# Linear attention followed by a gated feed-forward layer on one core: the kernel rewritten with one 512-token block per batch, larger loads, Silu, and an instruction order fixed by hand

## The chip, the cores and the metric

The kernel runs on one core of a Trainium2 chip. The metric is the device time of one execution in microseconds (us). Before the change the median of three runs was 443.9 us (439.84 to 444.03). A profile is one further execution, recorded by the hardware profiler. Its span runs from the first to the last instruction and is usually a little shorter than the timed execution. TensorE multiplies matrices (PE in the profile, and PEld for its weight loads), VectorE (DVE), ScalarE (ACT) and GpSimd (POOL) do the elementwise work, and SyncE (SP) issues the stores.

## The reference, cut to what matters

There are 8 batches, 8 heads, 576 tokens and 64 columns per head. So the feed-forward layer gets 8 x 576 = 4608 tokens of 512 columns, and works with 2048 hidden columns.

```python
def phi(x): return np.where(x > 0, x, np.exp(x) - 1.0) + 1.0
q_p, k_p = phi(q), phi(k)
kv  = np.einsum('bhsd,bhse->bhde', k_p, v)
z   = np.sum(k_p, axis=2)
num = np.einsum('bhsd,bhde->bhse', q_p, kv)
den = np.einsum('bhsd,bhd->bhs', q_p, z)[..., None] + 1e-06
x   = (num / den) transposed to tokens x 512      # abridged
h   = x @ w_in                                    # 512 -> 2048
g   = h * sigmoid(beta * h)                       # written out in the original
y   = g @ w_out                                   # 2048 -> 512, float32
```

phi(x) equals max(x, 0) + min(exp(x), 1). Both kernels use a form of this. Also, h * sigmoid(beta h) = silu(beta h) / beta. The changed kernel uses that.

## The kernel before

The kernel handles one batch of attention, then one block of 512 tokens of the feed-forward layer, and so on. Batches have 576 tokens and blocks 512, so a ninth block is left at the end. A scheduler orders the instructions of each engine. The parts that matter here:

```python
# weights: converted to bf16 by the DMA, issued on GpSimd's queue
nc.gpsimd.dma_start(out=w_in_sb, in_=moe_w_in...)
nc.gpsimd.dma_start(out=w_out_sb, in_=moe_w_out...)
...
# one load per 128 tokens and tensor: every written run is 64 columns of bf16, 128 bytes
nc.gpsimd.dma_start(out=qk[:sn, 0], in_=q_src[s0:s0 + sn])
...
# attention: per head pair and token tile one small normalization
nc.vector.reciprocal(rden[:sn], num_ps[:sn, :, D])
nc.vector.tensor_mul(xtile[:sn], num_ps[:sn, :, :D], rden_v)      # 128 x 128
nc.tensor.matmul(xtp[:, sc, :], xtile..., identity, is_transpose=True, ...)
...
# the block: two PSUM buffers for h_ps, two for y_ps
for ff in range(FFC):                                   # 16
    for kc in range(DMC): nc.tensor.matmul(h_ps, w_in_sb[...], xT_sb[...], ...)   # 4
    nc.scalar.activation(sig, h_ps, Sigmoid, scale=beta_sb[:, ff : ff + 1])
    nc.vector.tensor_mul(g_sb[:, ff, :], h_ps, sig)
for tsub in range(TB // P):                             # 4
    for ff in range(FFC): nc.tensor.matmul(y_ps, g_sb[...], w_out_sb[:, ff, :], ...)  # 16
    nc.vector.tensor_copy(y_sb, y_ps)
    nc.sync.dma_start(out=out[...], in_=y_sb)
```

Of the kernel before, what the change touches and what calls it, by code (L numbers as in the profile page):

```python
# [10 lines left out]
BF16 = mybir.dt.bfloat16  # L11


@with_exitstack
def kernel(
# [10 lines left out]
    nc = tc.nc  # L26

    B, H, S, D = q.shape
    DMODEL = H * D
    NTOK = B * S  # L30
    DFF = moe_w_in.shape[1]
    P = 128
    DMC = DMODEL // P
    FFC = DFF // P
    SC = (S + P - 1) // P
    SP = SC * P

    assert moe_w_in.shape == (DMODEL, DFF)
    assert moe_w_out.shape == (DFF, DMODEL)
    assert out.shape == (NTOK, DMODEL)  # L40
    assert DMODEL % P == 0 and DFF % P == 0

    consts = ctx.enter_context(tc.tile_pool(name="consts", bufs=1))

    identity = consts.tile([P, P], BF16)
    make_identity(nc, identity)

    w_in_sb = consts.tile([P, DMC, DFF], BF16)
    w_out_sb = consts.tile([P, FFC, DMODEL], BF16)
    beta_sb = consts.tile([P, FFC], F32)  # L50
    with tc.high_priority(offset=-100000):
        nc.gpsimd.dma_start(out=w_in_sb, in_=moe_w_in.rearrange("(c p) f -> p c f", p=P))
        nc.gpsimd.dma_start(out=w_out_sb, in_=moe_w_out.rearrange("(c p) f -> p c f", p=P))
        for ff in range(FFC):
            nc.sync.dma_start(out=beta_sb[:, ff : ff + 1],
                              in_=moe_beta[ff * P : (ff + 1) * P, None])

    kvmask = consts.tile([P, 2, D + 1], BF16)
    nc.gpsimd.memset(kvmask, 0.0)
    nc.gpsimd.memset(kvmask[:D, 0, :], 1.0)  # L60
    nc.gpsimd.memset(kvmask[D : 2 * D, 1, :], 1.0)

    xT_sb = consts.tile([P, DMC, NTOK], BF16)

    atp = ctx.enter_context(tc.tile_pool(name="attn", bufs=3))
    attn_batch = ctx.enter_context(tc.tile_pool(name="attn_batch", bufs=2))
    psA = ctx.enter_context(tc.tile_pool(name="psA", bufs=2, space=bass.MemoryType.PSUM))
    kvnps = ctx.enter_context(tc.tile_pool(name="kvnps", bufs=2, space=bass.MemoryType.PSUM))
    moe_sb = ctx.enter_context(tc.tile_pool(name="moe_sb", bufs=3))
    moe_g = ctx.enter_context(tc.tile_pool(name="moe_g", bufs=2))  # L70
    hps = ctx.enter_context(tc.tile_pool(name="hps", bufs=2, space=bass.MemoryType.PSUM))
    yps = ctx.enter_context(tc.tile_pool(name="yps", bufs=2, space=bass.MemoryType.PSUM))

    def phi_to(dst, src, tag):
        shape = list(src.shape)
        mn = atp.tile(shape, BF16, tag=tag + "_mn")
        nc.vector.tensor_scalar(mn, src, 0.0, None, mybir.AluOpType.min)  # L77
        ex = atp.tile(shape, BF16, tag=tag + "_ex")
        nc.scalar.activation(ex, mn, mybir.ActivationFunctionType.Exp)  # L79
        rl = atp.tile(shape, BF16, tag=tag + "_rl")  # L80
        nc.scalar.activation(rl, src, mybir.ActivationFunctionType.Relu)  # L81
        nc.vector.tensor_add(dst, rl, ex)  # L82

    def attention_batch(b):
        q_pT = attn_batch.tile([P, DMC, SP], BF16, tag="q_pT")
        qk_p_all = attn_batch.tile([P, SC, 2, DMODEL], BF16, tag="qk_p_all")
        v_all = attn_batch.tile([P, SC, H, D + 1], BF16, tag="v_all")
        nc.gpsimd.memset(v_all[:, :, :, D : D + 1], 1.0)

        q_src = q[b].rearrange("h s d -> s h d")  # L90
        k_src = k[b].rearrange("h s d -> s h d")
        v_src = v[b].rearrange("h s d -> s h d")

        for sc in range(SC):
            s0 = sc * P
            sn = min(P, S - s0)

            qk = atp.tile([P, 2, H, D], BF16, tag="qk")
            if sn < P:
                nc.gpsimd.memset(qk[sn:P], -50.0)  # L100
            nc.gpsimd.dma_start(out=qk[:sn, 0], in_=q_src[s0:s0 + sn])  # L101
            nc.gpsimd.dma_start(out=qk[:sn, 1], in_=k_src[s0:s0 + sn])  # L102
            qkv = qk.rearrange("p a h d -> p (a h d)")
            qk_p_sc = qk_p_all[:, sc].rearrange("p a f -> p (a f)")
            phi_to(qk_p_sc, qkv, tag="phi_qk")
            q_p = qk_p_all[:, sc, 0, :]
            tps = psA.tile([P, SC, P], BF16, tag="trps")
            for dmc in range(DMC):
                nc.tensor.matmul(  # L109
                    tps[:, dmc, :], q_p[:, dmc * P : (dmc + 1) * P], identity,  # L110
                    is_transpose=True, start=(dmc == 0), stop=(dmc == DMC - 1),
                    skip_group_check=True,
                )
            nc.vector.tensor_copy(q_pT[:, :, s0 : s0 + P], tps[:, :DMC, :])

            nc.gpsimd.dma_start(out=v_all[:sn, sc, :, :D], in_=v_src[s0:s0 + sn])  # L116
            if sn < P:
                nc.gpsimd.memset(v_all[sn:P, sc, :, :D], 0.0)
        k_p_all = qk_p_all[:, :, 1, :]

        tok0 = b * S
        for p in range(DMC):
            dlo = p * P
            kv01 = kvnps.tile([P, 2 * (D + 1)], F32, tag="kvn")
            for sc in range(SC):
                nc.tensor.matmul(
                    kv01,
                    k_p_all[:, sc, dlo : dlo + P],
                    v_all[:, sc, 2 * p : 2 * p + 2].rearrange("s h e -> s (h e)"),
                    start=(sc == 0),  # L130
                    stop=(sc == SC - 1),
                )

            kv_bd = atp.tile([P, 2, D + 1], BF16, tag="kv_bd")
            nc.vector.tensor_mul(kv_bd, kv01.rearrange("p (g e) -> p g e", g=2), kvmask)  # L135

            xtp = psA.tile([P, SC, P], BF16, tag="trps")
            for sc in range(SC):
                s0 = sc * P
                sn = min(P, S - s0)  # L140

                num_ps = kvnps.tile([P, 2, D + 1], F32, tag="kvn")
                nc.tensor.matmul(  # L143
                    num_ps.rearrange("p g e -> p (g e)"),
                    q_pT[:, p, s0 : s0 + P],
                    kv_bd.rearrange("p g e -> p (g e)"),
                    start=True,
                    stop=True,
                )
                rden = atp.tile([P, 2], F32, tag="rden")  # L150
                nc.vector.reciprocal(rden[:sn], num_ps[:sn, :, D])  # L151
                xtile = atp.tile([P, 2, D], BF16, tag="xtile")
                rden_v = rden[:sn, :, None].to_broadcast([sn, 2, D])
                nc.vector.tensor_mul(xtile[:sn], num_ps[:sn, :, :D], rden_v)  # L154
                if sn < P:
                    nc.vector.memset(xtile[sn:P], 0.0)
# [83 lines left out]
```

## Time and profile before

| | before |
|---|---|
| time, median | 443.9 us |
| span of the profile | 443.6 us |
| TensorE, VectorE, ScalarE busy | 77%, 57%, 54% |
| mean granted clock of TensorE | 0.942 |
| first h product / first copy of y | 59.7 / 112.5 us |
| DMA packets | 122,619, of which 115,424 under 512 B |

TensorE is the engine to watch. Its time goes in three ways: products that run at full rate, products that run at a reduced clock, and waits. The prediction below shows the lines. In a group line (the page's costliest groups), the parts are: source line, engine, operation, out<-in with shapes, count | busy us, mean ns | idle time before, and what ended most of it.

VectorE copies y out of PSUM four times per block, so the start of each block's last copy dates the end of that block. For the kernel before these ends are 125.3, 179.4, 209.6, 239.1, 295.3, 323.6, 365.1, 410.2 and 439.7 us.

### The profile page before, as it was taken

Reading aid. Unit: us, or ns where it says so; the run is one execution under the profiler, and the core shown is the slowest. Engines: PE = TensorE matmul, PEld = TensorE weight load, DVE = VectorE, ACT = ScalarE, POOL = GpSimd, SP = SyncE. Lnnn points to the kernel's source line nnn. Section 1 sums busy time; section 2 is a strip of 40 time slices with the busy share of each in tenths; the row PEclk is TensorE's granted clock in tenths of the full one; section 3 lists DMA queues with packets and bytes.
Section 4 is the critical chain, followed back from the end, with each engine's and each line's share of the span. In section 5 each row is a group of like instructions: output and inputs, shape, how many; then the busy total and the mean of one; then the engine's idle time right before and its main releaser. Section 6 shows DMA issues by size and latency. Waiting matters only on the chain.

```text
span 443.6 us, 5178 instructions
## 1 busy us (share of the span) xinstructions
PE 341.9 (77%) x1760; PEld 160.0 (36%) x1792; DVE 253.0 (57%) x716; ACT 238.2 (54%) x272; POOL 118.9 (27%) x155
## 2 busy tenths in 40 slices
PE   0256366377877768989998677899988997899996
PEld 0134123133343333434444333444434444244342
DVE  1699538408387687453554858735467537453551
ACT  2764539839789999740551998525103500341540
POOL 9998618202813463300002534000000000000000
PEclk9999999679989899999999988999979996699999
DMA  9999999917997497901002958020110010001002
GB/s 80 110 130 110 186 103 108 184 12 47 137 95 48 31 96 86 104 0 73 24 8 90 99 37 55 1 95 0 49 47 2 0 71 25 0 0 73 24 1 95
DMA packets 122619, 28.14 MB, mean 63 GB/s; under 512 B 115424, under 2 KB 117472, under 8 KB 122592
## 3 DMA queue, kind: packets, MB, share of 16 engines
q0 software_dynamic: 115104, 18.36, 57.1%
q1 hardware_dynamic: 7488, 9.45, 6.1%
q8 instruction: 14, 0.23, 0.2%
q14 instruction: 13, 0.11, 0.1%
HBM read 36.71 MB, written 9.44 MB: 104 GB/s over the span
## 4 chain that ended last, share of the span: by engine, by line
PE 55%; DMA 16%; DVE 15%; POOL 6%; issue 4%; ACT 4%; DVEq 0%; POOLq 0%; ACTq 0%
PE y_ps L193 26%; PE h_ps L176 25%; DMA qk<-in_k_dram 9%; DMA w_out_sb<-in_moe_w_out_dram 4%; DVE g_sb L188 3%; DMA w_in_sb<-in_moe_w_in_dram 3%; DVE xtile L154 3%; POOL qk L101 2%; POOL v_all L116 2%; DVE mn L77 2%; ACT sig L184 2%; DVE rden L151 2%; PE xtp L157 2%; DVE qk_p_all L82 1%; DVE xT_sb L162 1%
## 5 line engine op out<-in xcount | busy, mean ns | idle before, releaser
L184 ACT ACTIVATE sig<-h_ps,beta_sb 128x512 bf16<-128x512 f32 x144 | 96.6, 686 | 147.2 <-PE h_ps L176 134.9
L176 PE MATMUL h_ps<-xT_sb,w_in_sb 128*128 128x512 bf16 x554 | 150.2, 401 | 25.1 <-DVE g_sb L188 18.8
L193 PE MATMUL y_ps<-w_out_sb,g_sb 128*128 128x512 bf16 x566 | 143.2, 387 | 12.7 <-DMA w_out_sb<-in_moe_w_out_dram 9.7
L188 DVE TENSOR_TENSOR g_sb<-h_ps,sig 128x512 bf16<-128x512 f32 x144 | 96.8, 686 | 52.9 <-ACT sig L184 52.8
L176 PEld LDWEIGHTS <-w_in_sb 128*128 128x128 bf16 x576 | 57.9, 101 | 99.4 <-issue 44.1
L193 PEld LDWEIGHTS <-g_sb 128*128 128x128 bf16 x576 | 56.0, 100 | 84.5 <-issue 16.4
L157 PE MATMUL xtp<-identity,xtile 128*128 128x128 bf16 x160 | 35.3, 254 | 27.7 <-DVE xtile L154 26.9
L79 ACT ACTIVATE ex<-mn 128x1024 bf16<-128x1024 bf16 x40 | 41.8, 1053 | 20.6 <-DVE qk_p_all L82 10.7
L101 POOL DMA_DIRECT2D qk<-in_q_dram x40 | 34.8, 869 | 59.4 <-ACT rl L81 50.0
L201 DVE COPY y_sb<-y_ps 128x512 f32<-128x512 f32 x36 | 24.6, 689 | 45.5 <-PE y_ps L193 45.4
L81 ACT ACTIVATE rl<-qk 128x1024 bf16<-128x1024 bf16 x40 | 41.9, 1051 | 11.6 <-DMA qk<-in_k_dram 11.6
L154 DVE TENSOR_TENSOR xtile<-num_ps,rden 128x128 bf16<-128x128 f32 (+1 forms) x160 | 41.3, 283 | 1.1 <-DVE rden L151 0.2
L143 PE MATMUL num_ps<-kv_bd,q_pT 128*128 128x130 bf16 x160 | 32.3, 254 | 9.3 <-DVE kv_bd L135 9.3
L151 DVE RECIPROCAL rden<-num_ps 128x2 f32<-128x2 f32 (+1 forms) x160 | 22.1, 160 | 28.0 <-PE num_ps L143 26.1
L157 PEld LDWEIGHTS <-xtile 128*128 128x128 bf16 x160 | 16.5, 103 | 56.7 <-DVE xtile L154 47.2
L77 DVE TENSOR_SCALAR mn<-qk 128x1024 bf16<-128x1024 bf16 x40 | 20.2, 508 | 28.1 <-DMA qk<-in_k_dram 28.0
L116 POOL DMA_DIRECT2D v_all<-in_v_dram x40 | 35.7, 907 | 0.0
L109 PE MATMUL tps<-identity,qk_p_all 128*128 128x128 bf16 x160 | 17.8, 245 | 22.9 <-DVE qk_p_all L82 20.3
L102 POOL DMA_DIRECT2D qk<-in_k_dram x40 | 34.7, 867 | 1.3 <-DMA qk<-in_q_dram 0.8
L184 ACT ACT_TABLE_LOAD x24 | 30.8, 1283 | 4.9 <-PE h_ps L176 4.1
L82 DVE TENSOR_TENSOR qk_p_all<-rl,ex 128x1024 bf16<-128x1024 bf16 x40 | 26.9, 680 | 6.1 <-ACT ex L79 5.9
L79 ACT ACT_TABLE_LOAD x23 | 29.5, 1283 | 0.4
(23 smaller groups left out, 123.4 us busy)
## 6 DMA issues: line engine op xcount, KB each, us to landing
out_dram<-y_sb SPq DMA_DIRECT2D x36, 256.0 KB, 2.0
qk<-in_q_dram POOLq DMA_DIRECT2D x32, 128.0 KB, 4.3
qk<-in_k_dram POOLq DMA_DIRECT2D x32, 128.0 KB, 4.6
v_all<-in_v_dram POOLq DMA_DIRECT2D x32, 128.0 KB, 4.7
w_in_sb<-in_moe_w_in_dram POOLq DMA_DIRECT2D x1, 2048.0 KB, 13.9
w_out_sb<-in_moe_w_out_dram POOLq DMA_DIRECT2D x1, 2048.0 KB, 16.2
qk<-in_q_dram POOLq DMA_DIRECT2D x8, 64.0 KB, 3.6
qk<-in_k_dram POOLq DMA_DIRECT2D x8, 64.0 KB, 3.7
```

Of the source, the lines that this page charges most:

```text
L79: nc.scalar.activation(ex, mn, mybir.ActivationFunctionType.Exp)
L81: nc.scalar.activation(rl, src, mybir.ActivationFunctionType.Relu)
L101: nc.gpsimd.dma_start(out=qk[:sn, 0], in_=q_src[s0:s0 + sn])
L102: nc.gpsimd.dma_start(out=qk[:sn, 1], in_=k_src[s0:s0 + sn])
L116: nc.gpsimd.dma_start(out=v_all[:sn, sc, :, :D], in_=v_src[s0:s0 + sn])
L143: nc.tensor.matmul(num_ps.rearrange("p g e -> p (g e)"), q_pT[:, p, s0 : s0 + P], kv_bd.rearrange("p g e -> p (g e)"), start=True, stop=True,)
L154: nc.vector.tensor_mul(xtile[:sn], num_ps[:sn, :, :D], rden_v)
L157: nc.tensor.matmul(xtp[:, sc, :], xtile.rearrange("s g e -> s (g e)"), identity, is_transpose=True, start=(sc == 0), stop=(sc == SC - 1), ...
L176: nc.tensor.matmul(h_ps, w_in_sb[:, kc, ff * P : (ff + 1) * P], xT_sb[:, kc, t0 : t0 + TB], start=(kc == 0), stop=(kc == DMC - 1),)
L184: nc.scalar.activation(sig, h_ps, mybir.ActivationFunctionType.Sigmoid, scale=beta_sb[:, ff : ff + 1],)
L188: nc.vector.tensor_mul(g_sb[:, ff, :], h_ps, sig)
L193: nc.tensor.matmul(y_ps, g_sb[:, ff, tsub * P : (tsub + 1) * P], w_out_sb[:, ff, :], start=(ff == 0), stop=(ff == FFC - 1),)
```

## The change

The intent is to keep TensorE fed from the start:

- Each block is the first 512 tokens of one batch. The 64 odd tokens of all eight batches make the ninth block.
- The weights are loaded right after batch 0. q, k and v come in whole batches with written runs of 512 bytes (1 KB read).
- Silu writes g in one step, and 1/beta is multiplied into w_out once.
- h and y share four PSUM buffers.
- Normalization is done for 512 columns at once.
- The order of the instructions is written out by hand: generators hand out one step of the next batch's attention after each group of four large products.

The diff has 522 lines. This is its core (cuts marked with "..."):

```diff
+    ctx.enter_context(tc.manual_schedule())
+    mmps = ctx.enter_context(tc.tile_pool(name="mmps", bufs=4, space=bass.MemoryType.PSUM))
-    hps = ctx.enter_context(tc.tile_pool(name="hps", bufs=2, space=bass.MemoryType.PSUM))
-    yps = ctx.enter_context(tc.tile_pool(name="yps", bufs=2, space=bass.MemoryType.PSUM))
...
+        nc.gpsimd.dma_start(
+            out=dst[:, :, 0:NJ, :].rearrange("p h j d -> p h (j d)"),
+            in_=src[b, :, 0:MAIN, :].rearrange("h (p j) d -> p h (j d)", j=NJ),
+        )
...
-            sig = moe_sb.tile([P, TB], BF16, tag="sig")
-            nc.scalar.activation(
-                sig, h_ps, mybir.ActivationFunctionType.Sigmoid,
-                scale=beta_sb[:, ff : ff + 1],
-            )
-            nc.vector.tensor_mul(g_sb[:, ff, :], h_ps, sig)
+            nc.scalar.activation(
+                g[:, ff, :], hp, ACTF.Silu, scale=beta_c[:, ff : ff + 1]
+            )
+            step(fill)
...
-                nc.vector.reciprocal(rden[:sn], num_ps[:sn, :, D])
-                nc.vector.tensor_mul(xtile[:sn], num_ps[:sn, :, :D], rden_v)
+            nc.vector.tensor_scalar(den[:n], nv[:, :, :, D], 1e-6, None, ALU.add)
+            nc.vector.reciprocal(rden[:n], den[:n])
+            nc.vector.tensor_mul(
+                xs[t][:n], nv[:, :, :, 0:D],
+                rden[:n, :, :, None].to_broadcast([n, 2, 4, D]),
+            )
...
-    for b in range(B):
-        attention_batch(b)
-        moe_block(b)
-    moe_block(B)
+    h_phase(0, xT[0], [chain(wait(4), w_out_scale())])
+    clear_tail(2)
+    load_next(2)
+    f = chain(wait(6), lazy(elu, 1), wait(3), lazy(attention, 1))
+    y_phase(0, [f])
+    drain(f)
+    load_next(3)
+    h_phase(1, xT[1])
+    f = chain(lazy(elu, 2), lazy(attention, 2))
+    e3 = chain(wait(8), lazy(elu, 3))
+    y_phase(1, [f, e3])
...
+    for b in range(2, B + 1):
+        att = lazy(attention, b + 1) if b + 1 < B else wait(0)
+        h_phase(b, xT[b % 3] if b < B else xT_tail, [att])
+        load_next(b + 3)
+        e = lazy(elu, b + 2) if b + 2 < B else wait(0)
+        y_phase(b, [att, e])
```

The attention generator issues the transposes of tile t-2 in the same step as the q transposes of tile t, one group of h products after the numerators of tile t-2:

```python
        for t in range(NT + 2):
            if t < NT:
                q_trans(t)
            if t >= 2:
                x_trans(t - 2)
            yield
            if 1 <= t < NT + 1:
                numer(t - 1)
                yield
```

## The prediction

> **What bounds the kernel now.** I read the page's busy shares first, then the windows for clock and rate, the chain that ended last, the groups, and the timeline for the pitch of single operations.
>
> ```profile
> PE 341.9 (77%) x1760; PEld 160.0 (36%) x1792; DVE 253.0 (57%) x716; ACT 238.2 (54%) x272; POOL 118.9 (27%) x155
> PEclk9999999679989899999999988999979996699999
> ```
>
> TensorE is the busiest engine, yet its 77% is not work at full rate: durations overlap, include waiting in the pipe, and the clock row dips to 6. The windows (span, busy time with instruction count of PE, PEld, DVE, ACT and POOL, granted clock, DMA share, GB/s written) split the run:
>
> ```profile
> 0.00:32.00 32.00, 8.39 (x57) 4.92 (x57) 16.76 (x48) 17.69 (x18) 30.16 (x46) 1.00 1.77 109
> 32.00:60.00 28.00, 12.03 (x82) 7.27 (x83) 18.70 (x74) 13.08 (x14) 18.45 (x23) 1.00 1.57 148
> 60.00:92.00 32.00, 17.72 (x98) 8.73 (x98) 17.43 (x56) 23.87 (x25) 13.01 (x15) 0.84 1.23 116
> 210.00:246.00 36.00, 33.32 (x173) 15.13 (x175) 20.53 (x52) 16.18 (x21) 4.86 (x7) 1.00 0.20 44
> 328.00:388.00 60.00, 52.48 (x256) 24.14 (x261) 34.78 (x109) 14.72 (x22) 0.00 (x0) 0.81 0.05 18
> ```
>
> Three things show. The first 92 us hold almost no MoE work, while DMA is full. A dense stretch (210 to 246) gets clock 1.00. A stretch of sparse attention work (328 to 388) gets 0.81. Over the span 1 - 0.942 of 443.6 us, 26 us, is lost clock. The chain names the loads behind the late start:
>
> ```profile
> 45.35 13.87 DMA w_in_sb<-in_moe_w_in_dram
> 74.49 16.23 DMA w_out_sb<-in_moe_w_out_dram
> ```
>
> Issued behind several batches of q, k and v on the same GpSimd queue, the weights land at 59.2 and 90.7. Only then do the first h and y products run.
>
> ```profile
> L184 ACT ACTIVATE sig<-h_ps,beta_sb 128x512 bf16<-128x512 f32 x144 | 96.6, 686 | 147.2 <-PE h_ps L176 134.9
> L176 PE MATMUL h_ps<-xT_sb,w_in_sb 128*128 128x512 bf16 x554 | 150.2, 401 | 25.1 <-DVE g_sb L188 18.8
> L188 DVE TENSOR_TENSOR g_sb<-h_ps,sig 128x512 bf16<-128x512 f32 x144 | 96.8, 686 | 52.9 <-ACT sig L184 52.8
> L157 PE MATMUL xtp<-identity,xtile 128*128 128x128 bf16 x160 | 35.3, 254 | 27.7 <-DVE xtile L154 26.9
> L154 DVE TENSOR_TENSOR xtile<-num_ps,rden 128x128 bf16<-128x128 f32 (+1 forms) x160 | 41.3, 283 | 1.1 <-DVE rden L151 0.2
> L184 ACT ACT_TABLE_LOAD x24 | 30.8, 1283 | 4.9 <-PE h_ps L176 4.1
> ```
>
> Two rings starve TensorE: h waits 18.8 us for the multiply by sigmoid to free one of two PSUM buffers, and the x transposes wait 26.9 us for 160 little normalizations. Lastly the pitch of single products, cold and warm, and of a y group:
>
> ```profile
> 26.81 0.75 PE L126 MATMUL kv<-v_all,qk_p_all 128*128 128x130 bf16 x5
> 260.67 0.45 PE L126 MATMUL kv<-v_all,qk_p_all 128*128 128x130 bf16 x5
> ...
> 436.27 0.69 DVE L201 COPY y_sb<-y_ps 128x512 f32<-128x512 f32 x1 [2.76 <-PE y_ps L193]
> 439.72 0.69 DVE L201 COPY y_sb<-y_ps 128x512 f32<-128x512 f32 x1 [2.76 <-PE y_ps L193]
> ```
>
> Five products span 0.75 us early and 0.45 us later; with one alone at 0.32 and 0.22 us, the pitch is 107 ns cold and 57 ns warm. Two y copies lie 3.45 us apart for 16 products: 216 ns each.
>
> **What the Trainium skill says.** "TensorE: Matmul & The Clock Gate", section "Back-to-back issue gap": N/2.4 + 2.5 ns when warm, so 216 ns at 512 and 57 ns at 130 columns. The trace agrees. The same page, Part 1 (the HAM clock gate): half rate by default, full rate after some 3.4 us of sustained work. The trace agrees: eight h products from 381.17 take 3.57 us at half clock, and from 388 on the clock is full. "ScalarE: Activation LUTs", section "What ACT_TABLE_LOAD costs": 1283 ns a load, an ACTIVATE 186 ns + 0.833 ns per element. Trace: 1283 ns, and 1.04 to 1.06 us for 1024 elements. "VectorE: DVE Perf Modes", section "Side-by-side": bf16 at four elements a cycle for one source, two for two sources, some 150 cycles fixed. Trace: 1024 elements in 0.42 us at best (min with zero) and 0.68 us (add). No run here has 2560 elements yet; from these I estimate 0.81 and 1.48 us.
>
> **The change, part by part.** The arithmetic of TensorE stays: 1152 large products (144 x 4 for h, 36 x 16 for y) and 640 small ones. The floor is 1152 x 0.216 = 248.8 us plus 640 x 0.057 = 36.5 us, 285 us.
>
> - Removed: 144 multiplies of 686 ns on VectorE. Silu writes g directly, with 1/beta folded into w_out. The h ring is now four buffers and one 0.69 us ACTIVATE per 0.864 us of product, so TensorE no longer waits there.
> - Normalization: 160 pairs of reciprocal and multiply (22 + 41 us) become 40 groups of add, reciprocal and 512-wide multiply: 0.16 + 0.16 + 0.69 and two gaps of 0.04 = 1.09 us.
> - Table loads: 48 become about 17; Exp runs only in the y stage. ScalarE has slack.
> - Order: the instruction order of the built kernel shows that during the h stage of batch 2 to 6 one attention step of the next batch follows each four h products, and the phi of the batch after that lies in the y stage.
> - Loads: batch 0 only (1.77 MB written), then w_in, w_out in f32, then batch 1. w_in went at 151 GB/s written, windows beside it at 192.
>
> Working along the path:
>
> 1. Batch 0 loaded. k lands at about 7 us, v at 10, q at 13.5 (1.77 MB at 150 to 190 GB/s, from about 1.5, plus landing). Exp of q 2.3 us, min 0.8, add 1.5: q ready near 18.2.
> 2. Attention of batch 0 alone. Each token tile costs VectorE two 0.415 us copies and the 1.09 us chain; with the transposes between, cold, I make it 2.2 us a tile. Two mask multiplies, the first transposes and numerator until 22, four more tiles to 31, last copy: **32 us**. w_in (12 to 15 us after q) is there by then.
> 3. h of block 0: 13.8 us, plus 2 cold: 48. y of block 0: w_out in f32 lands around 43 to 49, 16 scalings of some 0.41 us (6.6 us) mostly earlier; 13.8 us plus 1 waiting: **63**.
> 4. Attention of batch 1: nearly all its steps come after y of block 0, with no large product beside them: 14 us: **77**.
> 5. h of block 1, nothing beside it, cold start: 15.8: **93**.
> 6. y of block 1 holds phi of batch 2, attention of batch 2 and phi of batch 3. VectorE then has two phis of 7.1 us (three ops per tensor 0.81 + 0.81 + 1.48, twice, plus the v copy 0.81), attention 11 us (2 x 0.69 + 10 x 0.415 + 5 x 1.09), four y copies 2.8: 28 us in order against 18.5 us of products. With its waits 30: **123**.
> 7. Blocks 2 to 6: 27.65 us of large products, 80 x 0.057 = 4.6, and waits of x transposes: the chain of 1.09 plus 0.3 latency is covered by 0.864 of h and 0.23 of q transposes in three tiles (0.24 short) and by 0.864 alone in two (0.46 short): 1.6. 33.9 x 5 = 169, plus 1 cold: **293**.
> 8. Blocks 7 and 8: 55.3: **348**. Last copy and store: TensorE stopped 3.9 us before the end before: **352**.
>
> The saving of 92 us is thus roughly 28 from h starting at 32 rather than 60, 17 from no standing before w_out, the rest from waits in the rings and lost clock, less some 25 in which batches 1 and 2 stand uncovered.
>
> **Rivals.** (a) TensorE is filled from the first product and hardly waits: steps 4 and 6 shrink to the length of their products: 325 to 335. For it: four PSUM buffers. Against it: one engine order, in which every attention product waits for VectorE. (b) VectorE becomes the bound in the steady blocks: 7.1 + 2.8 + 11 = 21 us per 33.9 us speaks against it; but in-order queueing (a y copy behind a min that waits for Exp) could add 2 us a block: 365. (c) The loads stay the bound: f32 w_out writes twice the bytes of before (4.2 MB), and if written bytes cap the rate at 150 to 190 GB/s, w_out takes 22 to 28 us rather than 12 to 16, lands at 55 to 60, and y of block 0 waits 8 to 10 us more: 362. For it: windows never exceed about 215 GB/s written. Against: the cast reads twice that, so reading is the likelier cap. (d) Throttling of the denser kernel: the dense window at 1.00 speaks against it; at 0.9 in the steady part it would cost 25: 377.
>
> **Range and chances.** The terms least sure are the start (3 either way), step 6 and step 4 (4 each), the waits per block (5), and (c) (up to 10, one-sided). That gives 352, and 334 to 370 for 8 in 10. For less than 2% gain some 83 us would have to be missing, more than all rivals but a broken overlap: faster 0.97, same 0.02, slower 0.01.
>
> **What would show it.** First h product near 32 and first y copy near 53; a hole of small products of about 14 us between y of block 0 and h of block 1; VectorE above 85% busy in y of block 1; after 125 us blocks 34 us apart, 27.7 for the last two; large products 216 ns apart and clock 1.00 there; no wait of h for ScalarE. It is wrong if the steady blocks show 38 us or more, if w_out lands past 55, or if the clock falls under 0.95 in dense blocks.

## The result, and the profile after

The changed kernel takes 357.87 us (median of 4 runs, 355.75 to 358.14). In the same rounds the kernel before took 443.96 (439.84 to 445.92). The ratio is 0.805, with a 95% interval of 0.800 to 0.810. A ratio here is the mean time of one kernel's fast runs over that of the other's fast runs of the same rounds, so it is not quite the ratio of the medians. The profiled execution: a span of 355.9 us.

The page of the changed kernel, busy shares and clock:

```profile
PE 307.2 (86%) x1793; PEld 153.5 (43%) x1793; DVE 167.0 (47%) x341; ACT 153.2 (43%) x174; POOL 47.8 (13%) x64
PEclk9999999759999699999999999999999999999998
```

VectorE has lost 86 us of work and more than half of its instructions. TensorE's busy share has gone up from 77% to 86%, although its busy time went down. The mean clock is 0.967. By the prediction's measure (1 - 0.967) x 355.9 = 12 us are lost to the clock, where before it was 26. That measure is rough. It counts slow time in which TensorE has no work, and it misses the start: these views show 1.00 there, yet 20 kv products from 14.77 us take 2.35 us, some 107 ns each, the pitch that the prediction calls cold. The dips that are left while TensorE has work, in the 8th and 9th and in the 14th slice, lie in the hole of batch 1's attention and where batch 2's ends.

Five stretches from the windows (span, busy time with count of PE, PEld, DVE, ACT and POOL, granted clock, DMA share, GB/s written):

```profile
0.00:32.06 32.06, 10.07 (x81) 7.85 (x82) 20.14 (x49) 7.24 (x4) 17.74 (x28) 1.00 1.18 204
62.30:75.24 12.94, 6.95 (x69) 5.00 (x67) 9.93 (x28) 0.00 (x0) 0.67 (x1) 0.65 1.27 178
91.50:121.04 29.54, 20.27 (x146) 10.84 (x144) 23.19 (x42) 11.21 (x6) 8.60 (x10) 0.94 1.00 136
192.41:226.67 34.26, 33.25 (x209) 16.67 (x208) 19.32 (x38) 18.01 (x20) 0.00 (x0) 1.00 0.09 32
322.83:350.50 27.67, 27.63 (x129) 12.31 (x126) 2.77 (x5) 10.99 (x16) 0.00 (x0) 1.00 0.16 39
```

They are: the start until attention of batch 0 is done, the hole in which batch 1's attention stands alone, y of block 1 with batches 2 and 3 mixed in, one steady block (block 4, with the attention of batch 5 and the phi of batch 6), and block 8 alone. The 1.00 of the first row is the blind spot just named. In the hole TensorE is busy for 6.95 of 12.94 us, at clock 0.65. In the last two rows it is busy practically throughout, at clock 1.00.

The groups that answer to the two rings of the prediction (h, and the x transposes):

```profile
L275 ACT ACTIVATE g<-h_ps,beta_c 128x512 bf16<-128x512 f32 x144 | 98.5, 687 | 120.6 <-PE h_ps L271 119.9
L271 PE MATMUL h_ps<-xT,w_in 128*128 128x512 bf16 x512 | 128.6, 392 | 0.0
L241 PE MATMUL xtp<-identity,xs 128*128 128x128 bf16 (+1 forms) x160 | 17.0, 237 | 20.9 <-DVE xs L231 18.8
...
L231 DVE TENSOR_TENSOR xs<-nps,rden 128x512 bf16<-128x512 f32 (+1 forms) x40 | 27.6, 689 | 1.4
```

The h products' idle time before them, 25.1 us in the kernel before, is 0.0. In these lines ScalarE waits for TensorE, and not the other way round. Silu costs the same 0.69 us as Sigmoid did. The wait of the x transposes has only gone from 26.9 to 18.8 us. That is the ring that remains.

The chain that ended last (start, length, what):

```profile
5.35 9.07 DMA xqk<-in_q_dram
...
32.13 15.64 PE h_ps L271 x64
47.77 6.92 PE y_ps L296 x32
...
75.24 16.28 PE h_ps L271 x64
...
336.65 13.83 PE y_ps L296 x64
```

The weights are no longer in the chain: their place is taken by q of batch 0, and from 32 us on the chain is mostly TensorE (65% of the whole span). The exceptions are the hole, where it alternates between VectorE and TensorE, and y of block 1, where it runs through an Exp of ScalarE and then through VectorE (20% of the span in all). In the last line 64 products take 13.83 us, 216 ns each, the full rate. h of block 1, from 75.24, takes 2.5 us more than that, because the hole before it let the clock fall.

Where the 87.7 us of span went, from the ends of the blocks:

| stretch | before | after | change |
|---|---|---|---|
| start to end of block 0 | 125.3 | 62.3 | -63.0 |
| blocks 1 and 2 | 84.3 | 98.3 | +14.0 |
| blocks 3 to 6 | 155.5 | 134.6 | -20.9 |
| blocks 7 and 8 | 74.6 | 55.3 | -19.3 |
| last copy of y to the end of the span | 3.9 | 5.4 | +1.5 |

The rows do not carry the same attention work in both kernels (the old one was further ahead with attention by block 2), so this table says where in time the difference lies, not which part of the change made it. The experiments do that.

Lastly, the timeline of one x transpose in a steady block (start, length, engine, what, and in brackets the idle time before and who ended it):

```profile
200.88 0.40 PE L220 MATMUL nps<-kv_bd,q_pT 128*128 128x130 bf16 x4
...
201.31 0.17 DVE L228 TENSOR_SCALAR den<-nps 128x8 f32<-128x8 f32 x1 [0.67 <-PE nps L220]
...
202.49 0.23 PEld L241 LDWEIGHTS <-xs 128*128 128x128 bf16 x4 [0.31 <-DVE xs L231]
```

From den to the end of xs VectorE takes 201.31 to 202.44, 1.13 us. TensorE has one group of four h products and the q transposes to run in that time, and is 0.31 us short. In a block this adds up to about 2 us: 34.26 less 27.65 of large products and 4.6 of small ones.

### The profile page after: what moved, and what is told of

It reads as the page before. It is cut to its first block, busy times and chain, and to the rows that moved or that the text cites. A ratio compares the mean times of both kernels' runs of the same rounds, so it can differ in the third digit from the quotient of the medians.

```text
span 355.9 us, 4500 instructions
## 1 busy us (share of the span) xinstructions
PE 307.2 (86%) x1793; PEld 153.5 (43%) x1793; DVE 167.0 (47%) x341; ACT 153.2 (43%) x174; POOL 47.8 (13%) x64
## 2 busy tenths in 40 slices
DMA packets 46133, 30.19 MB, mean 85 GB/s; under 512 B 13840, under 2 KB 40480, under 8 KB 46112
## 4 chain that ended last, share of the span: by engine, by line
PE 65%; DVE 20%; issue 5%; DMA 4%; ACT 3%; POOL 1%; ACTq 0%; DVEq 0%; POOLq 0%
PE h_ps L271 30%; PE y_ps L296 25%; DVE xs L231 8%; PE xtp L241 5%; PE nps L220 3%; DMA xqk<-in_q_dram 3%; DVE rden L229 2%; ACT e L152 2%; DVE e L155 2%; DVE den L228 2%; DVE y_sb L303 2%; DMA out_dram<-y_sb 2%; PE kvp L191 1%; DVE qk_p L156 1%; DVE xT L249 1%
## 5 line engine op out<-in xcount | busy, mean ns | idle before, releaser
L275 ACT ACTIVATE g<-h_ps,beta_c 128x512 bf16<-128x512 f32 x144 | 98.5, 687 | 120.6 <-PE h_ps L271 119.9
L271 PE MATMUL h_ps<-xT,w_in 128*128 128x512 bf16 x512 | 128.6, 392 | 0.0
L296 PE MATMUL y_ps<-w_out,g 128*128 128x512 bf16 x576 | 127.3, 379 | 0.0
L296 PEld LDWEIGHTS <-g 128*128 128x128 bf16 x576 | 56.0, 98 | 65.8
L271 PEld LDWEIGHTS <-w_in 128*128 128x128 bf16 x576 | 54.1, 100 | 55.3 <-issue 6.2
L152 ACT ACTIVATE e<-xqk 128x2560 bf16<-128x2560 bf16 x16 | 36.7, 2331 | 4.6 <-DMA xqk<-in_q_dram 3.1
L241 PE MATMUL xtp<-identity,xs 128*128 128x128 bf16 (+1 forms) x160 | 17.0, 237 | 20.9 <-DVE xs L231 18.8
L275 ACT ACT_TABLE_LOAD x7 | 9.0, 1283 | 51.1 <-PE h_ps L271 51.1
L231 DVE TENSOR_TENSOR xs<-nps,rden 128x512 bf16<-128x512 f32 (+1 forms) x40 | 27.6, 689 | 1.4
L156 DVE TENSOR_TENSOR qk_p<-r,e 128x2560 bf16<-128x2560 bf16 x16 | 23.9, 1492 | 0.5
L241 PEld LDWEIGHTS <-xs 128*128 128x128 bf16 (+1 forms) x160 | 9.7, 105 | 31.3 <-DVE xs L231 31.3
L209 PE MATMUL qtp<-identity,qk_p 128*128 128x128 bf16 (+1 forms) x160 | 15.8, 227 | 6.8 <-DVE kv_bd L197 5.0
L209 PEld LDWEIGHTS <-qk_p 128*128 128x128 bf16 (+1 forms) x160 | 11.9, 104 | 16.3 <-issue 7.6
L220 PE MATMUL nps<-kv_bd,q_pT 128*128 128x130 bf16 (+1 forms) x160 | 18.3, 244 | 0.3 <-DVE q_pT L213 0.2
```

The lines of the kernel that those rows point to most:

```text
L152: nc.scalar.activation(e, x, ACTF.Exp)
L156: nc.vector.tensor_add(st[b, "p"][:, a].rearrange("p j (h d) -> p h j d", h=H), r, e)
L209: nc.tensor.matmul(tp[:, p, :n], qk_p[:n, 0, t, p * P : (p + 1) * P], identity[:n, :n], is_transpose=True, start=True, stop=True, skip_gro ...
L220: nc.tensor.matmul(nps[:n, p // 2, o : o + 2 * (D + 1)], q_pT[:, p, t * P : t * P + n], kv_bd[:, p, :], start=True, stop=True, skip_group_ ...
L231: nc.vector.tensor_mul(xs[t][:n], nv[:, :, :, 0:D], rden[:n, :, :, None].to_broadcast([n, 2, 4, D]),)
L241: nc.tensor.matmul(tp[:, p, :n], xv[:n, p * P : (p + 1) * P], identity[:n, :n], is_transpose=True, start=True, stop=True, skip_group_check ...
```

## The experiments

Twelve kernels ran. All outputs are right. Kernels "from the changed kernel" undo or extend one part of it, and those "from the kernel before" add one part alone. My theory was: most of the gain comes from TensorE no longer waiting in the ring of h (Silu in place of sigmoid and multiply, and four buffers), the early start of h gives the next part, and the load shape gives little. The rival was that the early weights carry it: then the kernel before should gain most of the time by a mere move of two loads. No run put the late weights into the new order, so what the early start is worth there was not measured apart.

| label | from | edit | time, us | ratio |
|---|---|---|---|---|
| e1_sigmul | changed | Sigmoid and multiply again | 392.1 | 0.880 |
| e2_mm2 | changed | 2 PSUM buffers | 367.9 | 0.826 |
| e3_sigmul_mm2 | changed | both | 422.0 | 0.947 |
| e4_256B | changed | short runs in the loads | 361.8 | 0.812 |
| e5_xlate | changed | x transposes one group later | 349.4 | 0.781 |
| e6_early1 | changed | batch 1 mixed into block 0 | 345.0 | 0.772 |
| e8_ysb4 | changed | 4 buffers for y_sb | 356.7 | 0.798 |
| e7_all | changed | e5, e6 and e8 together | 331.7 | 0.742 |
| e9_pool_scale | e7_all | scaling of w_out on GpSimd | 341.5 | 0.771 |
| b1_order | before | weights right after batch 0 | 455.0 | 1.022 |
| b2_silu | before | Silu and scaled w_out | 426.1 | 0.960 |
| b3_order_silu | before | both | 444.3 | 0.998 |

The median of the kernel before was 445.3 to 446.4 us in these rounds. In e9_pool_scale the interval of the ratio, 0.768 to 0.775, lies far below 1.

### Putting sigmoid, multiply and two buffers back

e1_sigmul:

```diff
-            nc.scalar.activation(g[:, ff, :], hp, ACTF.Silu, scale=beta_c[:, ff : ff + 1])
+            sig = work.tile([P, 512], BF16, tag="sig", name="sig")
+            nc.scalar.activation(sig, hp, ACTF.Sigmoid, scale=beta_s[:, ff : ff + 1])
+            nc.vector.tensor_mul(g[:, ff, :], hp, sig)
...
-    nc.vector.reciprocal(rbeta, beta_c)
+    nc.vector.memset(rbeta, 1.0)
```

> The changed kernel with Silu undone: Sigmoid on ScalarE and a multiply on VectorE, four PSUM buffers kept. My theory: in h stages without attention nothing changes (0.69 us on each engine per 0.864 us of products), but in the h stages of blocks 2 to 6 VectorE gets 16 x 0.69 = 11 us on top of 11.6 us of attention in about 20 us, and in its one queue every normalization waits behind a multiply: 4 to 6 us a block more, 378 to 388 us. Rival: with four buffers the multiply is hidden and Silu is worth nothing: under 362 us.

It took 392.1 us, some 34 more than the changed kernel, a little above the range. Blocks 7 and 8, which carry no attention, still take 27.6 us: with four buffers the extra step of VectorE costs TensorE nothing by itself. Blocks 4 to 6 take 39.6 rather than 34.3, and block 0 ends 8 us later. (In block 0 the multiplies queue behind the scalings of w_out, 1.66 us for four, so y starts at 55.6 rather than 47.6.) For the steady blocks the timeline of this kernel shows why:

```profile
263.85 0.40 PE L220 MATMUL nps<-kv_bd,q_pT 128*128 128x130 bf16 x4
...
264.77 0.69 DVE L279 TENSOR_TENSOR g<-h_ps,sig 128x512 bf16<-128x512 f32 x1 [0.81 <-ACT sig L276]
...
265.38 0.16 DVE L228 TENSOR_SCALAR den<-nps 128x8 f32<-128x8 f32 x1
...
266.55 0.23 PEld L241 LDWEIGHTS <-xs 128*128 128x128 bf16 x4 [1.34 <-DVE xs L231]
```

VectorE waits for a sigmoid (0.81 us) with the multiply at the head of its queue, although the numerators lie ready. Only then does the normalization start. The x transposes come 2.7 us after the numerators rather than 1.6, and TensorE waits for them for 1.34 us. VectorE is only 66% busy over the span, and 72% in a steady block (28.4 of 39.6 us). By this trace it is its order that holds TensorE, not its load. No run changed the order alone.

e2_mm2:

```diff
-    mmps = ctx.enter_context(tc.tile_pool(name="mmps", bufs=4, space=bass.MemoryType.PSUM))
+    mmps = ctx.enter_context(tc.tile_pool(name="mmps", bufs=2, space=bass.MemoryType.PSUM))
```

> The changed kernel with two PSUM buffers in place of four, Silu kept. My theory: the ring of two is 0.864 + 0.2 + 0.69 + 0.05 us = 1.80 us for two groups against 1.73 of products, so 0.6 us per h stage: 359 to 365 us. Rival: the buffers are what freed TensorE, not the missing multiply: over 375 us.

It took 367.9 us, 10 more than the changed kernel and somewhat above the range. Blocks without attention take 28.7 us (+1.1). Note that two buffers are fewer than the kernel before had: there h and y had two each, here they share the two.

e3_sigmul_mm2 makes both edits:

> Both undone: Sigmoid and multiply, two PSUM buffers. My theory: the ring takes 0.864 + 0.2 + 0.69 + 0.05 + 0.69 + 0.05 = 2.5 us for two groups, 1.26 us a group, 0.4 us more for 144 groups, part of it beside small products: 398 to 418 us, much more than the two single edits add up to. Rival: the effects add (under 390).

It took 422.0 us, again above the range. The two edits alone cost 34 and 10, together 64. With two buffers the four h products of 0.864 us no longer cover the round of ScalarE, VectorE and the semaphores between them: blocks without attention now take 34.0 us, which is 6.4 more, or 0.4 for each of the 16 groups of h. In blocks with attention it is 41.3. The view of waits of this kernel, which has no such line in the changed one:

```profile
PE h_ps L271 <- DVE g L279: 18.0, 40, 1.2
```

So in the new order Silu and the four buffers together are worth 64 of some 87 us. What is left of the rewrite without them, 422.0 against 445.3, is 23. Both figures are for this comparison: with h and y sharing two buffers, e3_sigmul_mm2 has less room than the kernel before.

### One part alone in the kernel before

b2_silu:

```diff
-            sig = moe_sb.tile([P, TB], BF16, tag="sig")
-            nc.scalar.activation(sig, h_ps, Sigmoid, scale=beta_sb[:, ff : ff + 1])
-            nc.vector.tensor_mul(g_sb[:, ff, :], h_ps, sig)
+            nc.scalar.activation(g_sb[:, ff, :], h_ps, Silu, scale=beta_sb[:, ff : ff + 1])
...
+    nc.vector.reciprocal(rbeta, beta_sb)
+    for ff in range(FFC):
+        nc.vector.tensor_scalar(w_out_sb[:, ff, :], w_out_sb[:, ff, :],
+                                rbeta[:, ff : ff + 1], None, mybir.AluOpType.mult)
```

> The kernel before with Silu and w_out scaled by 1/beta, nothing else. My theory: the 18.8 us of h waiting for the multiply go, and the normalizations no longer queue behind 97 us of multiplies: 415 to 430 us. Rival: the start and the attention chain bind, and Silu alone is worth under 5 us: over 438 us.

It took 426.1 us, within the range. The ratio of 0.960 has an interval of 0.946 to 0.974, all of it a gain of over 2%, although the verdict on record is "unclear". But this was not Silu alone. The scaling reads w_out early, and the scheduler then issued the load of w_out 15 us earlier. First the kernel before, then this one:

```profile
74.49 1.15 POOL L53 DMA_DIRECT2D w_out_sb<-in_moe_w_out_dram  x1
```

```profile
59.54 1.17 POOL L53 DMA_DIRECT2D w_out_sb<-in_moe_w_out_dram  x1
```

The first y product runs at 77.9 rather than 90.8, and block 0 ends at 105.5 rather than 125.3. The eight blocks after it take 312.4 against 314.4 us. So 20 of the 22 us of span are gained in block 0, and how much of that is Silu's and how much the earlier w_out's is not separated by any run.

Put side by side, this gives the most useful reading. Silu in the old order, with its two h buffers (and w_out earlier): 0.960. The new order with sigmoid, multiply and two buffers (e3): 0.947. If these two multiplied, the new order with Silu and two buffers would give 0.91. It gives 0.826 (e2). Nearly half of that gain (8 of 17 points) comes only from the pair. My reading is that a fast ring needs an order that always has the next product ready, and the order needs a ring that does not stop it. The multiplying is rough, since the buffers differ (two and two before, two shared here).

b1_order:

```diff
     with tc.high_priority(offset=-100000):
-        nc.gpsimd.dma_start(out=w_in_sb, in_=moe_w_in.rearrange("(c p) f -> p c f", p=P))
-        nc.gpsimd.dma_start(out=w_out_sb, in_=moe_w_out.rearrange("(c p) f -> p c f", p=P))
...
+        if b == 0:      # in attention_batch, after the loads of batch 0
+            nc.gpsimd.dma_start(out=w_in_sb, ...)
+            nc.gpsimd.dma_start(out=w_out_sb, ...)
```

> The kernel before with one thing changed: the weight loads issued right after the loads of batch 0 instead of behind batches 1 and 2. My theory: the first h product moves from 59.7 to about 37 us and y no longer waits for w_out (9.7 us of wait, some 17 us on the chain), but the loads of batch 1 come later and take some of it back: 415 to 430 us. Rival: the wait only moves to the later batches: over 438 us.

It took 455.0 us, 2% longer than the kernel before (ratio 1.022, 1.005 to 1.038; verdict on record unclear). The weights did come early: the first h product moved from 59.7 to 29.4 us, the first y copy from 112.5 to 92.5, and block 0 ended at 103.7 rather than 125.3. But blocks 1 and 3 then took 65.7 and 69.6 us, so those 22 us were given back and more. ScalarE's timeline shows a new wait, in block 0:

```profile
42.27 1.06 ACT L79 ACTIVATE rl<-qk 128x1024 bf16<-128x1024 bf16 x1 [20.42 <-DMA qk<-in_k_dram]
43.23 1.04 ACT L77 ACTIVATE ex<-mn 128x1024 bf16<-128x1024 bf16 x1
44.29 1.28 ACT L185 ACT_TABLE_LOAD   x1
45.59 1.26 ACT L185 ACTIVATE sig<-h_ps,beta_sb 128x512 bf16<-128x512 f32 x2
46.87 1.28 ACT L77 ACT_TABLE_LOAD   x1
```

The loads of batch 1 now stand behind the weights. ScalarE has a piece of batch 1 at the head of its queue and stands for 20.42 us, while h products wait for their sigmoids behind it. Then it alternates between the two functions, with a table load of 1.28 us for each one or two operations. This wait took part of block 0's gain. The loss came later, and why is not shown: block 1 has 18 table loads, but the kernel before has 17 in its block 1. What the windows show in blocks 1 and 3 is a lower clock, 0.84 and 0.88, against 0.94 in blocks 1 and 4 of the kernel before, its slow ones. In this order, then, moving the loads alone did not help.

b3_order_silu makes both edits, with the scaling of w_out placed after batch 0:

> The kernel before with both of its single edits: weights loaded right after batch 0, and Silu with 1/beta in w_out. The early weights alone gained nothing (455 us against 446), Silu alone gave 426. My theory: an early start is lost again because the engine queues tie h of block 0 to the phi of batch 1, whose loads the weights now delay, whatever the activation: 420 to 432 us, as Silu alone. Rival: the early start was eaten by the ring of h, and with Silu it pays the 15 to 20 us by which the first y copy came earlier: under 412 us.

It took 444.3 us (6 runs, 440.47 to 448.2). The ratio of the fast runs is 0.998 (0.986 to 1.009), and the verdict is left at unclear. Neither my range nor that of the rival came true: the early weights cancel Silu's gain here too. Its first h product is at 32.9 us, as early as in the changed kernel, yet blocks 1 and 3 take 65.9 and 59.5 us. The profile of this kernel fell in a slow execution (clock 0.908), so I do not explain it in detail. Whether the same wait as in b1_order does it is not shown.

### The shape of the loads

e4_256B:

```diff
-        nc.gpsimd.dma_start(
-            out=dst[:, :, 0:NJ, :].rearrange("p h j d -> p h (j d)"),
-            in_=src[b, :, 0:MAIN, :].rearrange("h (p j) d -> p h (j d)", j=NJ),
-        )
+        for j in range(NJ):
+            nc.gpsimd.dma_start(
+                out=dst[:, :, j, :],
+                in_=src[b, :, j * P : (j + 1) * P, :].rearrange("h p d -> p h d"),
+            )
```

The token order of the store is changed to fit. This brings back the 256-byte runs read (128 written) of the kernel before.

> The changed kernel with token j*128+p in place of 4p+j on a partition, so that every run of the q, k, v loads is 256 bytes and there are four main loads per tensor instead of one. My theory: batch 0 takes 15 issues of 0.7 to 0.9 us (13 us) instead of 6 (5 us), so q lands about 3.5 us later and h starts at 35 to 36 instead of 32; w_out lands 5 to 8 us later and y of block 0 may wait a few us; the rest is hidden: 361 to 367 us. Rival: the loads bind the whole run when packets are small: over 375 us. Rival 2: nothing at all (under 359).

It took 361.8 us, as expected. The packets went from 46,133 to 121,014, and the first Exp of q started at 17.16 rather than 14.50 us. But h started at 37.0 rather than 32.1, later than I expected. About half of that is not the loads landing later. GpSimd has 15 loads to issue before it builds the identity that the transpose of beta needs, and VectorE's phi stands behind beta in its queue. First the changed kernel, then this one:

```profile
7.02 0.29 PE L131 MATMUL bps<-ident,beta_row 16*128 16x16 f32 x1 [7.02 <-POOL ident masks.py:199]
```

```profile
14.91 0.28 PE L132 MATMUL bps<-ident,beta_row 16*128 16x16 f32 x1 [14.91 <-POOL ident masks.py:199]
```

VectorE's first maximum of phi starts at 16.28 rather than 8.36. Later blocks take the same time as in the changed kernel, but for block 2, which is 1.6 us shorter. So the load shape is worth about 4 us, all of it at the start. How much of it is the short runs and how much the number of issues is not separated.

### The waits that were left

e5_xlate issues the x transposes of a tile one group of h products later:

```diff
-            if t >= 2:
-                x_trans(t - 2)
-            yield
-            if 1 <= t < NT + 1:
-                numer(t - 1)
-                yield
+            yield
+            if t == 0:
+                continue
+            if t >= 2:
+                x_trans(t - 2)
+            if t < NT + 1:
+                numer(t - 1)
+            yield
```

> The changed kernel with the transposes of x moved one group of h products later. My theory: the 2 us a block by which TensorE waits for the normalization go away in the five blocks that hold attention in their h stage, blocks 34.3 to about 32.3 us: 346 to 350 us. Rival: the wait only moves to another operation of the chain, or VectorE is the limit there: over 355 us.

It took 349.4 us, as expected. The view of waits (who waits for what: total us, times, longest) of the changed kernel and then of this one:

```profile
PEld L241 <- DVE xs L231: 31.3, 40, 1.8
```

```profile
PEld L241 <- DVE xs L231: 17.3, 14, 1.7
```

Of the 40 tiles only 14 still wait (the ten of batches 0 and 1 have no large products beside them). A steady block takes 32.6 us. Large and small products add up to 32.25, so hardly any wait is left in it.

e8_ysb4 gives y_sb four buffers:

```diff
-            y_sb = work.tile([P, DM], F32, tag="y_sb", name="y_sb")
+            y_sb = work.tile([P, DM], F32, tag="y_sb", name="y_sb", bufs=4)
```

> The changed kernel with four y_sb buffers in place of two. In blocks 2 and 3 VectorE stands 2.3 and 3.4 us for a store to land while the next batch is loaded, and TensorE then waits 0.95 us. My theory: 1 to 3 us, 355 to 357 us. Rival: none, the stores are hidden (over 357.5).

It took 356.7 us (356.01 to 356.92). That is within the range, but 1 us less is not clear of the scatter: the changed kernel's own four runs, from other rounds, lie between 355.75 and 358.14. The line that suggested it is in VectorE's timeline of the changed kernel:

```profile
160.63 0.69 DVE L303 COPY y_sb<-y_ps 128x512 f32<-128x512 f32 x1 [3.42 <-DMA out_dram<-y_sb]
```

A copy waits 3.42 us for a store to leave its buffer, while the loads of a whole batch run (the chain shows this store at 6.26 us, where the median is 2.3). This happens three times, 6.1 us in all. Most of it cost TensorE nothing.

e6_early1 loads batch 1 before w_out and mixes its attention into h of block 0, and moves batch 2 one block forward (the diff is cut to its core):

```diff
+    load_k(1)
+    load_q(1)
+    load_v(1)
     for i in range(4):
         nc.gpsimd.dma_start(out=w_out_f[i], in_=w_out_v[:, i * 4 : (i + 1) * 4, :])
-        if i == 1:
-            load_q(1)
-            load_k(1)
-    load_v(1)
...
-    h_phase(0, xT[0], [chain(wait(4), w_out_scale())])
+    drain(elu(1))
+    att = chain(wait(5), lazy(attention, 1))
+    sc = chain(wait(9), w_out_scale())
+    h_phase(0, xT[0], [att, sc])
...
-    for b in range(2, B + 1):
+    for b in range(1, B + 1):
```

> The changed kernel with batch 1 loaded before w_out, its phi done before h of block 0, its attention beside h and y of block 0, and so every later batch one stage earlier. My theory: the hole of 12.9 us after y of block 0 shrinks to its 4.6 us of products (8 us), y of block 1 goes from 29.5 to 14 us and the attention of batch 2 costs 6.5 us in h of block 1 instead (11 us net less 2 us), and two cold restarts of some 2 us go: 334 to 342 us. Rival: w_out or the loads of batch 2 now come too late and y of block 0 waits: over 348 us.

It took 345.0 us, above the range. The hole is gone: blocks 1 and 2 take 36.1 and 35.0 rather than 53.6 and 44.7 us, which is 27.2 less. But block 0 now ends at 76.1 rather than 62.3, and takes back 13.8. Of this, 4.6 are batch 1's small products, which had to go somewhere. The timeline, of VectorE's scalings and the x transposes alone, shows where most of the rest comes from:

```profile
51.10 1.67 DVE L328 TENSOR_SCALAR w_out<-xqk,rbeta 128x512 bf16<-128x512 f32 x4
51.24 0.40 PE L240 MATMUL xtp<-identity,xs 128*128 128x128 bf16 x4 [2.29 <-DVE xs L230]
...
56.55 0.40 PE L240 MATMUL xtp<-identity,xs 128*128 128x128 bf16 x4 [2.73 <-DVE xs L230]
```

Each step of the scaling is four operations, 1.67 us, and stands in VectorE's queue ahead of batch 1's attention. TensorE waits 2.29 and 2.73 us for x, and from 57.4 to 60.8 the clock is low. Part of the gain was turned into a new wait, of the same kind as in e1_sigmul.

e7_all joins e5, e6 and e8:

> Both edits and four y_sb buffers. If the three are independent: 20 us from batch 1, 2 us a block in seven attentions, and 2 us from the stores: 318 to 328 us. If they share a cause (the same waits): 330 or more.

It took 331.7 us (331.12 to 332.28), with a ratio of 0.742 (0.739 to 0.745). It beats both kernels. It is above the range that I gave, and at the value that I gave for gains that are shared: e5, e6 and e8 alone saved 8.4, 12.8 and 1.1 us, 22.4 in sum, and together they saved 26. So they did not take from each other. The surplus fits the number of steady blocks: each is 1.66 us shorter (34.27 to 32.61), and e7_all has seven where e5_xlate has five. It was my range that rested on e6's expected time, not on its measured one. TensorE in its page:

```profile
PE 297.7 (90%) x1793; PEld 151.3 (46%) x1793; DVE 164.7 (50%) x341; ACT 153.2 (47%) x174; POOL 46.8 (14%) x64
```

Its span is 329.2 us at clock 0.99. As an estimate, the least time in this design is the 31.8 us before the first h product, 248.8 us of large products, 4.6 us of small ones for each of the seven other batches, and the last 5.4 us: 318.2. So some 11 us of waits are left, nearly all in block 0, which takes 42.3 us (from 31.8 to 74.2) for 32.25 us of products.

e9_pool_scale tries to remove that wait, with the scaling moved to GpSimd and begun as soon as w_out lands:

```diff
-                nc.vector.tensor_scalar(
+                nc.gpsimd.tensor_scalar(
                     w_out_sb[i][:, c, :], w_out_f[i][:, c, :], rbeta[:, ff : ff + 1],
                     None, ALU.mult,
                 )
...
+    drain(w_out_scale())
-    h_phase(0, xT[0], [att, sc])
-    drain(sc)
+    h_phase(0, xT[0], [att])
```

> All edits of the best kernel so far (331.7 us), with the 16 scalings of w_out on GpSimd instead of VectorE, where each stood 1.6 us in front of the attention of batch 1 and TensorE waited 2 to 3 us for it. If the queue of VectorE in block 0 was the cause: y of block 0 ends 4 to 7 us earlier, 324 to 328 us. If w_out now comes too late, or GpSimd holds up the loads of batch 2: 331 us or more.

It took 341.5 us, 10 more than e7_all, and both halves of the second branch came true. First VectorE's line in the changed kernel, then GpSimd's in this one:

```profile
32.37 3.25 DVE L329 TENSOR_SCALAR w_out<-g,rbeta 128x512 bf16<-128x512 f32 x8
```

```profile
37.78 13.38 POOL L330 TENSOR_SCALAR w_out<-g,rbeta 128x512 bf16<-128x512 f32 x8 [8.85 <-DMA g<-in_moe_w_out_dram]
```

Eight operations take 13.38 us rather than 3.25, and the last of the sixteen ends at 63.4. So w_out comes late: h of block 1 starts at 76.8 rather than 72.6, 4.2 us later. And the loads of batch 2 stand behind the scalings in GpSimd's queue: their first issue moves from 52.23 to 63.42. ScalarE waits for them, and TensorE then waits for the phi of batch 2 in h of block 1:

```profile
72.51 1.28 ACT L151 ACT_TABLE_LOAD   x1 [21.13 <-DMA xqk<-in_k_dram]
82.13 1.16 PE L190 MATMUL kvp<-vaug,qk_p 128*128 128x130 bf16 x10 [4.28 <-DVE qk_p L155]
```

By the last y copy block 0 ends at 85.9 us rather than 74.2, although TensorE was through with it at 76.8. Blocks 1 to 8 take the same time as in e7_all or less (block 1: 30.1 against 31.3). I did not try the scaling in single operations on VectorE, or on ScalarE.

## Why the prediction was right, and where a term was off

The time of 357.9 us lies within the range and 6 us above the predicted 352. (1.8 us of this is what a timed execution here takes beyond its span, 357.73 against 355.9; the steps add up a span.) No step failed outright. By the prediction's steps:

- **Step 1**, q ready near 18.2: 19.2. The k and q Exp started at 9.1 and 14.5. The estimates for 2560 elements, made from the 1024-element rows and from what the skill's page "VectorE: DVE Perf Modes", section "Side-by-side", says, were 0.81 and 1.48 us. They measured 0.835 and 1.492.
- **Step 2**, 32: 32.06. Here two errors cancel: q was ready 1 us late, and the attention took 12.9 rather than 13.8 us. The reciprocal takes 0.20 and not 0.16 us, so the chain is 1.13 rather than 1.09.
- **Step 3**, 48 and 63: 47.6 and 62.3. The last piece of w_out landed at 42.4, so rival (c), the loads stay the bound, fell.
- **Step 4**, a hole of 14 us until 77: 12.9, until 75.2, at clock 0.65. Rival (a) fell here: in one engine order, every attention product does wait for VectorE.
- **Step 5**, 15.8 us: 16.3. The clock stood at 0.85 in it.
- **Step 6**, 30 us until 123: 29.5, until 121.0. The sign that I named for it was wrong: VectorE is 79% busy here (23.19 of 29.54), not above 85%. I had added the full durations of operations that overlap a little back to back, and some of the phi had already run beside h of block 1. I had also left out that VectorE first stands until ScalarE's first Exp is done, 4.4 us into the stretch:

```profile
95.91 0.83 DVE L155 TENSOR_SCALAR e<-e 128x2560 bf16<-128x2560 bf16 x1 [18.87 <-ACT e L152]
```

  Nearly 5 us too much work and some 4 us of a wait that I had not seen cancel, so that 29.5 came so close to 30 is in part luck. That VectorE bounds the rest of the stretch was right.
- **Step 7** is the mis-sized term: 170 us predicted for blocks 2 to 6, 174.2 measured. Waits of x transposes were put at 1.6 us a block and are 2.0. Blocks 2 and 3 take 35.7 and 35.4 (from start of h to start of h) rather than 34.3: in block 2, h starts cold and y copies wait for stores, and the late last copy then costs TensorE 0.95 us in block 3. I had not thought of the stores there. I had priced the stores only at the end.
- **Step 8**, 55.3: 27.62 + 27.67. The tail was put at 3.9 as in the kernel before, and is 5.4: the odd tokens of two batches share each tile of the ninth block, so each tile needs two stores. That these are the reason for the 1.5 us is likely, but no run tests it.
- Rivals (b) and (d) fell: the steady blocks take 34.3 us, and the clock is 1.00 in them. Table loads were 14, not about 17.
- The section "Back-to-back issue gap" of the Trainium skill's page "TensorE: Matmul & The Clock Gate", which the prediction cites, gives its formula for an isolated product's gap, and 131 ns for a sustained stream of products of 512 columns. The sustained stream here ran at 216 ns (64 in 13.83 us), so the trace sides with the formula.

Two readings of the old profile were rough as well: the 26 us of lost clock (the result section says why), and a phi of 7.1 us, whose terms add up to 7.0.

What failed is the sentence after the steps, which split the saving into "roughly 28 from h starting at 32 rather than 60, 17 from no standing before w_out, the rest from waits in the rings and lost clock". That was read off the profile of the kernel before as if its waits could be removed one at a time. b1_order took away both of these first waits (h starts at 29.4, y at 92.5 rather than 112.5 to its first copy) and was 2% slower. e3_sigmul_mm2 kept the early start, put back sigmoid, multiply and two buffers, and lost 64 of the 87 us. The path sum gave the right total because it followed the new kernel's own path and did not rest on that split.

## What to carry to other kernels

Predict a rewrite by walking the path of the new order stage by stage, not by adding up the waits of the old profile: here Silu in the old order was worth 4% (with w_out moved along by the scheduler), the new order without it 5%, and the two together 17%. An engine far below full use can still hold up TensorE through the order of its queue, so keep long or late-released operations from standing ahead of short ones that TensorE is waiting for. When an early load or a filled hole brings less than its length, look for a wait that took its place, at the queue that now comes first. And where a scheduler orders the instructions, check what else an edit moved before you call it a single edit: b2_silu moved the load of w_out by 15 us.

## What the Trainium skill lacked or had wrong

- "TensorE: Matmul & The Clock Gate", Part 1 (the HAM clock gate), tells modellers that the ramp penalty is under 1% of a typical kernel's span. For one ramp this fits: h of block 0 took 15.64 us in the changed kernel, 1.8 us over full rate, 0.5% of the span. It must not be read as the whole cost of the clock in a kernel that mixes dense and sparse stretches: h of block 1 took another 2.5 us over full rate after the hole at 62 us (clock 0.65).
- "ScalarE: Activation LUTs", section "What ACT_TABLE_LOAD costs": the 1283 ns of the load agree, but the drain of some 1380 ns that it adds for every switch is not seen. ScalarE in the changed kernel:

```profile
47.81 0.69 ACT L275 ACTIVATE g<-h_ps,beta_c 128x512 bf16<-128x512 f32 x1 [0.18 <-PE h_ps L271]
48.51 1.28 ACT L152 ACT_TABLE_LOAD   x1
49.80 4.56 ACT L152 ACTIVATE e<-xqk 128x2560 bf16<-128x2560 bf16 x2
```

  Silu ends at 48.50, the load runs from 48.51 to 49.79, and Exp begins at 49.80: a switch costs 1.3 us, not 2.66. No page says whether Silu and Exp can share a table; in this kernel there are 7 loads before Silu and 7 before Exp, so here they did not.
- "GPSIMD Engine Reference", section 4.1 ("Engine selection"), calls operations of one input on GpSimd roughly line-rate. The scaling of 128x512 elements from f32 to bf16 took 1.67 us each on GpSimd (13.38 / 8) and 0.41 us each on VectorE (3.25 / 8), four times as long. (The times of GpSimd in a profile are rough, but these operations follow each other 1.54 us apart.)
- No page that I read says what happens to TensorE when one engine's queue mixes operations that other engines wait for with operations that themselves wait: in e1_sigmul, where the trace shows this, a steady block took 5.3 us more, with VectorE 72% busy in it.
